# Seven-product MLPs: VectorE takes GpSimd's arithmetic, GpSimd issues the stores, four products share a pair of banks

## The chip, the cores and the metric

The kernel runs on one core of a Trainium2 chip. The core has a matrix engine (TensorE, PE in the rows; PEld is its weight load), three engines for elementwise work (VectorE, DVE; ScalarE, ACT; GpSimd, POOL) and SyncE (SP), which only issues transfers. TensorE writes its sums to banks of PSUM, from where VectorE and ScalarE take them to SBUF. Each engine works through its own list of instructions in order; an instruction that has to wait holds up all behind it on that engine, transfers it issues among them. The metric is the time of one execution in microseconds. Three executions before took 1092.06, 1092.88 and 1094.47 us.

## The reference

Causal attention (4 batches, 8 heads, 576 positions, 64 per head) gives x of 2304 tokens by 512. Two MLPs follow, the second on the output of the first:

```python
def _moe_ref(x, w_in, w_out):          # 512 -> 2048 -> 512
    h = x @ w_in
    r = np.maximum(h, 0.0)
    g = r * r
    return (g @ w_out).astype(np.float32)

def _moe2_ref(x, w_in, w_out):         # 512 -> 2048 -> 512
    h = x @ w_in
    g = np.maximum(0.01 * h, h)        # leaky, slope 0.01
    return (g @ w_out).astype(np.float32)
```

The weights are given as 64-bit floats, inputs and output otherwise as 32-bit ones.

## The kernel before

There are five stages: attention with the first product of the first MLP (`up1`, plain) running beside and behind it, then three stages by seven products: `down` (g by w_out of MLP 1), `up` (by w_in of MLP 2) and `out` (by w_out of MLP 2).

**Seven products.** A block of 512 by 512 weights and a block of 512 rows by 768 tokens are each seen as 2 by 2 sub-blocks, and seven products of sums and differences of sub-blocks take the place of eight. Tokens go in three super-blocks (sb) of 768; the 2048-wide dimension goes in four quarters q. In `down` and `out` the loop is sb, product, q: the four q add up in PSUM, so a product is closed after four steps. In `up` it is sb, q, product: each product is closed after one step. A step is one call of `multiply` (L800): 12 matmuls of 384 columns in `down` and `up`, 18 of 256 in `out` (L792 in the rows). Each operand and each weight is cut into a rounded part and a rest, hence three passes.

**Operands.** `Operands.make` (L884) makes the operand of a step: ScalarE rounds (L889), VectorE forms the rest (L890), 768 elements in each of 128 partitions. Behind some products the sub-blocks are combined for later ones: L892 and L895 on VectorE, L894 and L897 on GpSimd, so four subtractions for each (sb, q) beside the seven rests. `down` makes three steps ahead (LEAD), in a ring of four buffers.

**Weights.** A 64-bit weight becomes a 32-bit one in `convert`: load into `wst` (SP, L140 or L142), L111 and L113 on ScalarE, L112 on VectorE, an integer addition L115 on GpSimd, L116 on VectorE, store to `wscr` (SP, L170). `wst` has one buffer in each stage, so the next load waits for L116. `arrive` reads four sub-blocks back, forms sums on GpSimd (L203 to L212) and cuts them for the products (L182 ScalarE, L183 VectorE). These are jobs that are started at numbered ticks, one tick for each step: the 16 conversions for `up` every third tick of `down`, those for `out` every second tick of `up`.

**Outputs.** `Outputs.done` (L840) is called when a product is closed. A product adds into a pair of banks, CHAIN says which: products 1 and 2 share one pair, 5 and 3 one, 7 and 4 one, 6 has its own. For each group of seven, ScalarE copies twice from PSUM (L844, L856) and VectorE adds five times (L848 to L863), and in `up` VectorE applies the slope to each of four outputs (L868). The stores (L955, L961, L966) are issued by SP, as all loads are. There are four pairs of banks, handed out in turn.

**Order.** A scheduler lays each engine's instructions in the order of its own estimate of the times; matmuls keep the order of the program. The buffers of a stage lie on those of the stage before in the order in which `open_pools` names them, and a buffer waits for what lay there. In `out` the first operand takes `dop1`, which lies on `cpost`, the buffers from which the last outputs of `up` are stored.

## Time and profile before

| | us |
|---|---|
| median of three executions | 1092.88 |
| the profiled execution | 1096.18 |
| its span, first to last instruction | 1094.3 |
| PE busy | 980.6 (90%) |
| DVE busy | 805.9 (74%) |
| ACT busy | 586.7 (54%) |
| POOL busy | 417.6 (38%) |

The matmuls of `down` begin at 459.4 us, those of `up` at 683.4, those of `out` at 903.0, and the last ends at 1089.9. Attention and `up1` fill what lies before. A busy share says little here, since every engine is in a different place of the program in each stage: the stages are read one by one, and in each the question is what PE waited for. In rows of waits, `A <- B` means that engine A stood idle until B ended.

### The profile page before, as it was taken

The numbers are of one execution on the slowest core, as the hardware profiler recorded it, in microseconds if no ns is written. First come the engines' busy times: TensorE is split into PE (matmuls) and PEld (weight loads), VectorE is DVE, ScalarE is ACT, GpSimd is POOL, SyncE is SP. The second block draws the span as 40 slices with busy tenths as digits, with TensorE's granted clock in tenths as the row PEclk, the third lists the DMA queues.
The fourth block names the chain that finished last, engine by engine and source line by source line (L and its number), as shares of the span: only waits on it lengthen the run. The fifth ranks groups of instructions, "written<-read, shape, count | busy, mean of one in ns | idle before, by whom it ended". The sixth has DMA issues, their size and how long they took to land.

```text
span 1094.3 us, 17158 instructions
## 1 busy us (share of the span) xinstructions
PE 980.6 (90%) x6056; PEld 886.3 (81%) x6056; DVE 805.9 (74%) x1299; ACT 586.7 (54%) x1149; POOL 417.6 (38%) x393
## 2 busy tenths in 40 slices
PE   5988999999999998889798787988988949999998
PEld 4766777888788777879688687887988949999998
DVE  6688776855777343396976979899688986696874
ACT  5577787877888566554444435443233433434432
POOL 4466555322552043234523434453123531232320
PEclk9899999999999999999999999999998988999999
DMA  7554747352745567757448243666757662624401
GB/s 138 120 127 117 174 148 176 111 144 65 179 149 167 196 223 260 254 182 255 134 151 278 91 159 126 216 216 200 238 164 237 215 207 84 208 72 140 150 3 57
DMA packets 206413, 178.53 MB, mean 163 GB/s; under 512 B 101460, under 2 KB 182356, under 8 KB 206328
## 3 DMA queue, kind: packets, MB, share of 16 engines
q1 hardware_dynamic: 193072, 158.26, 49.0%
q10 hardware_dynamic: 13256, 19.18, 4.8%
q8 instruction: 48, 0.79, 0.3%
q14 instruction: 37, 0.30, 0.1%
HBM read 111.25 MB, written 66.13 MB: 162 GB/s over the span
## 4 chain that ended last, share of the span: by engine, by line
PE 35%; DVE 24%; DMA 18%; issue 10%; ACT 8%; POOL 2%; SPq 1%; ACTq 0%; DVEq 0%; POOLq 0%
PE q L792 20%; PE h L602 7%; DMA wst<-in_moe_w_in_dram 6%; DVE op L890 6%; DMA wst<-in_moe_w_out_dram 4%; PE tr L514 3%; DVE wt L116 3%; DMA wb<-wscr 3%; DVE post L868 2%; DVE w L183 2%; PE tr L474 2%; PE S L424 2%; DVE t L440 2%; ACT wst L113 1%; ACT t L464 1%
## 5 line engine op out<-in xcount | busy, mean ns | idle before, releaser
L792 PE MATMUL q<-op,w 128*128 128x384 f32 x2016 | 375.6, 345 | 57.3 <-DVE op L890 30.5
L792 PEld LDWEIGHTS q<-op,w 128*128 128x128 f32 x2016 | 359.5, 193 | 73.3 <-DVE op L890 39.5
L890 DVE TENSOR_TENSOR op<-gp,op 128x768 fp32r<-128x768 f32 x189 | 234.5, 1255 | 53.3 <-ACT op L889 53.2
L602 PE MATMUL h<-xs,w 128*128 128x512 f32 (+1 forms) x960 | 232.1, 386 | 15.5 <-ACT r L588 6.8
L889 ACT ACTIVATE op<-gp 128x768 fp32r<-128x768 f32 x189 | 154.3, 841 | 161.0 <-PE q L792 121.9
L602 PEld LDWEIGHTS h<-xs,w 128*128 128x128 f32 x960 | 164.0, 195 | 47.2 <-ACT r L588 9.6
L792 PE MATMUL q<-w,op 128*128 128x256 f32 x1512 | 185.1, 286 | 13.2 <-ACT op L889 11.4
L792 PEld LDWEIGHTS q<-w,op 128*128 128x128 f32 x1512 | 184.1, 194 | 14.3 <-ACT op L889 11.7
L115 POOL TENSOR_TENSOR wt<-wt,wst 128x512 uint32<-128x512 uint32 x64 | 90.3, 1412 | 204.6 <-ACT wst L113 143.2
L111 ACT ACTIVATE wt<-wst 128x512 f32<-128x512 f32 x64 | 42.7, 667 | 139.1 <-DMA wst<-in_moe_w_in_dram 82.8
L897 POOL TENSOR_TENSOR gp<-gp 128x768 f32<-128x768 f32 x27 | 59.7, 2223 | 108.8 <-DVE op L890 105.0
L464 ACT ACTIVATE t<-t,m 128x128 f32<-128x128 f32 (+2 forms) x144 | 83.4, 580 | 32.5 <-DVE m L440 30.3
L894 POOL TENSOR_TENSOR gp<-gp 128x768 f32<-128x768 f32 x27 | 61.9, 2299 | 79.7 <-DVE gp L892 40.1
L112 DVE TENSOR_SCALAR wt<-wt 128x512 uint32<-128x512 uint32 x64 | 34.6, 541 | 68.3 <-ACT wt L111 68.3
L440 DVE CUSTOM_DVE_ANT_0 t<-S,mask 128x128 f32<-128x128 f32 (+2 forms) x129 | 57.7, 476 | 22.1 <-PE S L424 12.5
L474 PE MATMUL tr<-ident,t 128*128 128x128 f32 x384 | 67.4, 286 | 5.2 <-ACT t L464 3.2
L739 DVE TENSOR_TENSOR pT<-tr,pT 128x384 fp32r<-128x384 f32 (+2 forms) x96 | 51.6, 550 | 22.7 <-ACT pT L732 22.2
L474 PEld LDWEIGHTS tr<-ident,t 128*128 128x128 f32 x384 | 46.4, 144 | 21.5 <-issue 5.2
L116 DVE SCALAR_TENSOR_TENSOR wt<-wst,wt 128x512 uint32<-128x512 uint32 x64 | 51.7, 808 | 14.0 <-POOL wt L115 14.0
L868 DVE SCALAR_TENSOR_TENSOR post<-post 128x768 f32<-128x768 f32 x48 | 59.2, 1242 | 0.3
L732 ACT ACTIVATE pT<-tr 128x384 fp32r<-128x384 f32 (+4 forms) x108 | 51.1, 485 | 13.9 <-PE tr L474 11.6
L387 POOL TENSOR_TENSOR Y<-yt,Y 128x576 fp32r<-128x576 f32 x30 | 43.0, 1441 | 26.2 <-ACT Y L386 26.0
(103 smaller groups left out, 1225.7 us busy)
## 6 DMA issues: line engine op xcount, KB each, us to landing
gp<-gscr SPq DMA_DIRECT2D x48, 384.0 KB
qscr<-post SPq DMA_DIRECT2D x48, 384.0 KB
gp<-qscr SPq DMA_DIRECT2D x48, 384.0 KB
wst<-in_moe_w_in_dram SPq DMA_DIRECT2D x32, 512.0 KB
gscr<-gs ACTq DMA_DIRECT2D x32, 512.0 KB
wst<-in_moe_w_out_dram SPq DMA_DIRECT2D x32, 512.0 KB
wscr<-wt SPq DMA_DIRECT2D x48, 256.0 KB
wb<-wscr SPq DMA_DIRECT2D x40, 256.0 KB
```

The costliest lines, as they stand in the source:

```text
L115: nc.gpsimd.tensor_tensor(t, t, lw, ALU.add)
L116: nc.vector.scalar_tensor_tensor(t, hw, 0xC0000000, t, ALU.bitwise_and, ALU.bitwise_or)
L440: return nc.vector.tensor_tensor_reduce(t[:, a:z], sc, msk, -QK_SCALE, first, ALU.add, ALU.min, m).ins
L464: done = nc.scalar.activation(t[:, a:z], t[:, a:z], AF.Exp, bias=m[:, c:c + 1], scale=-1.0, accum_out=sums[:, s0:s0 + 1])
L474: nc.tensor.transpose(tr[:, c * P:(c + 1) * P], t[:, c * P:(c + 1) * P], ident)
L602: nc.tensor.matmul(h[:, :w], win[fc][:, a, c * P:(c + 1) * P], xs[j, c][:, z, :w], start=(c == 0 and y == 0), stop=(c == KC - 1 and y == 2))
L792: i = nc.tensor.matmul(*args, skip_group_check=True, **kw).ins
L868: nc.vector.scalar_tensor_tensor(t[1], t[1], 0.01, t[1], ALU.mult, ALU.max)
L889: a = nc.scalar.activation(t[:, 0], src, AF.Copy)
L890: c = nc.vector.tensor_tensor(t[:, 1], src, f32(t[:, 0]), ALU.subtract)
L894: nc.gpsimd.tensor_tensor(b[0, 1], b[1, 1], b[0, 1], ALU.subtract)
L897: nc.gpsimd.tensor_tensor(b[1, 0], b[1, 0], b[0, 0], ALU.subtract)
```

## The change

In the three stages by seven products, GpSimd no longer computes: the subtractions for operands, those for weights and the integer addition of `convert` go to VectorE, the stores of outputs and converted weights and one weight load in each `arrive` go from SP to GpSimd. The products are taken in another order and with other intermediate sums: 1, 7, 6, 2, 5, 4, 3. Products 1, 6, 5 and 3 now add into one pair of banks one after another, 7 and 4 into a second, 2 into a third; after 1, 6 and 7 ScalarE copies the state so far, after 2, 5 and 4 VectorE adds the copy, after 3 ScalarE takes the result. The slope is an activation of ScalarE. Conversions start every fourth tick in `down` (14 of them) and every third in `up` (18), and the buffers of `up` and `out` are named in another order: the first operand of `out` now lies on `cwa`, where weights are staged in `up`. The functions `convert` and `arrive` also make the weights of `down` beside attention and `up1` (16 conversions, 4 arrivals), so their additions, sums and stores move there as well.

```diff
-    ORDER = (1, 5, 6, 7, 2, 3, 4)
-    CHAIN = {1: 0, 2: 0, 5: 1, 3: 1, 6: 2, 7: 3, 4: 3}
-    FIRST = (1, 5, 6, 7)
-    EARLY = (1, 5, 6, 7)
+    ORDER = (1, 7, 6, 2, 5, 4, 3)
+    CHAIN = {1: 0, 6: 0, 5: 0, 3: 0, 7: 1, 4: 1, 2: 2}
+    FIRST = (1, 7, 2)
+    EARLY = (1, 7, 6, 5)
...
-    def words(t, st):
+    def words(t, st, adder=nc.gpsimd):
...
-        nc.gpsimd.tensor_tensor(t, t, lw, ALU.add)
+        adder.tensor_tensor(t, t, lw, ALU.add)
...
-    def convert(mat, ch, stage):
+    def convert(mat, ch, stage, adder=nc.vector):
...
-        yield from words(t, st)
-        yield
-        nc.sync.dma_start(wscr[mat][ch], f32(t))
+        for _ in words(t, st, adder):
+            pass
+        yield
+        nc.gpsimd.dma_start(wscr[mat][ch], f32(t))
...
-        def fetch(t, m, k):
+        def fetch(t, m, k, queue=nc.sync):
...
-            nc.sync.dma_start(t, wscr[mat][4 * q + b:4 * q + 4:2, :, h * 2 * P:(h + 1) * 2 * P]
+            queue.dma_start(t, wscr[mat][4 * q + b:4 * q + 4:2, :, h * 2 * P:(h + 1) * 2 * P]
...
         yield
         yield
         for i in ORDER:
-            if i == 5:
-                nc.gpsimd.tensor_tensor(s, c, u, ALU.add)
-                nc.gpsimd.tensor_tensor(c, a, c, ALU.subtract)
+            if i == 7:
+                nc.vector.tensor_tensor(s, c, u, ALU.add)
+                nc.vector.tensor_tensor(c, a, c, ALU.subtract)
             if i == 6:
-                nc.gpsimd.tensor_tensor(s, s, a, ALU.subtract)
-            if i == 7 and (keep or 2 in products):
-                fetch(a, 0, 1)
-            if i == 2:
+                nc.vector.tensor_tensor(a, s, a, ALU.subtract)
+            if i == 2 and (keep or 2 in products):
+                fetch(c, 0, 1, nc.gpsimd)
                 yield
-                if keep or 3 in products:
-                    nc.gpsimd.tensor_tensor(s, a, s, ALU.subtract)
+            if i == 3 and (keep or 3 in products):
+                nc.vector.tensor_tensor(c, c, a, ALU.subtract)
             if i not in products:
                 continue
             w = weight_tile(mat, i, q)
-            cut([w[:, z] for z in range(2)], {1: a, 5: s, 6: s, 7: c, 2: a, 3: s, 4: u}[i])
+            cut([w[:, z] for z in range(2)], {1: a, 7: c, 6: a, 2: c, 5: s, 4: u, 3: c}[i])
             yield
         if keep:
             yield
-            nc.sync.dma_start(sscr[q], s.rearrange("p c e -> p (c e)"))
+            nc.gpsimd.dma_start(sscr[q], c.rearrange("p c e -> p (c e)"))
     def arrive_kept(i, stage):
...
-        opens, closes = i in FIRST, i not in (1, 5, 7)
+        opens = i in FIRST
...
-            self.acc, self.ended = {}, []
+            self.acc, self.kept, self.ended = {}, {}, []
...
+        def leak(self, out, src):
+            nc.scalar.activation(out, src, AF.Prelu, alpha=0.01)
...
-            if i == 1:
-                self.s1, s1 = self.temp()
-                nc.scalar.activation(s1, x, AF.Copy)
-                self.s1v = s1
-            elif i == 6:
-                self.u2 = self.temp()
-                nc.vector.tensor_tensor(self.u2[1], y, self.s1v, ALU.add)
-                self.s5 = self.temp()
-                nc.vector.tensor_tensor(self.s5[1], z, self.u2[1], ALU.add)
-            elif i == 7:
-                nc.vector.tensor_tensor(self.s5[1], w, self.s5[1], ALU.add)
-                self.end(where, 1, 1, self.s5)
-            elif i == 2:
+            acc = self.view(self.acc[CHAIN[i]])
+            if i in (1, 6, 7):
                 t = self.temp()
-                nc.scalar.activation(t[1], x, AF.Copy)
-                self.end(where, 0, 0, t)
+                nc.scalar.activation(t[1], acc, AF.Copy)
+                self.kept[i] = t
             elif i == 3:
                 t = self.temp()
-                nc.vector.tensor_tensor(t[1], z, self.u2[1], ALU.add)
-                self.end(where, 0, 1, t)
-            elif i == 4:
-                nc.vector.tensor_tensor(self.u2[1], w, self.u2[1], ALU.add)
-                self.end(where, 1, 0, self.u2)
-        def end(self, where, m, h, t):
-            if self.kind == "up":
-                nc.vector.scalar_tensor_tensor(t[1], t[1], 0.01, t[1], ALU.mult, ALU.max)
-            self.ended.append((self.finish, where, m, h, t[0], t[1]))
+                if self.kind == "up":
+                    self.leak(t[1], acc)
+                else:
+                    nc.scalar.activation(t[1], acc, AF.Copy)
+                self.ended.append((self.finish, where, 0, 1, *t))
+            else:
+                t = self.kept.pop({2: 1, 5: 7, 4: 6}[i])
+                nc.vector.tensor_tensor(t[1], acc, t[1], ALU.add)
+                if self.kind == "up":
+                    self.leak(t[1], t[1])
+                self.ended.append((self.finish, where, {2: 0, 5: 1, 4: 1}[i], {2: 0, 5: 1, 4: 0}[i], *t))
     class Operands:
...
         def make(self, sb, q, i):
             b = {(k, h): self.part[sb, q, k, h] for k in range(2) for h in range(2)}
-            src = {1: b[0, 0], 5: b[0, 0], 6: b[0, 0], 7: b[0, 1], 2: b[1, 0], 3: b[1, 1], 4: b[1, 0]}[i]
+            src = b[{1: (0, 0), 7: (0, 1), 6: (0, 1), 2: (1, 0), 5: (0, 0), 4: (1, 0), 3: (1, 1)}[i]]
+            if i == 7:
+                nc.vector.tensor_tensor(b[0, 1], b[1, 1], b[0, 1], ALU.subtract)
             t = self.new(i)
             with tc.high_priority():
                 a = nc.scalar.activation(t[:, 0], src, AF.Copy)
                 c = nc.vector.tensor_tensor(t[:, 1], src, f32(t[:, 0]), ALU.subtract)
             if i == 1:
                 nc.vector.tensor_tensor(b[0, 0], b[0, 1], b[0, 0], ALU.subtract)
-            if i == 5:
-                nc.gpsimd.tensor_tensor(b[0, 1], b[1, 1], b[0, 1], ALU.subtract)
-                nc.vector.tensor_tensor(b[0, 0], b[1, 1], b[0, 0], ALU.subtract)
+            if i == 7:
+                nc.vector.tensor_tensor(b[0, 1], b[1, 1], b[0, 0], ALU.subtract)
             if i == 2:
-                nc.gpsimd.tensor_tensor(b[1, 0], b[1, 0], b[0, 0], ALU.subtract)
+                nc.vector.tensor_tensor(b[1, 0], b[1, 0], b[0, 1], ALU.subtract)
             self.op[sb, q, i] = t
             return a.ins, c.ins
...
-                    nxt = {2: (0, 0), 7: (0, 1), 3: (1, 1), 4: (1, 0)}.get(mi)
+                    nxt = {5: (0, 0), 2: (0, 1), 3: (1, 1), 4: (1, 0)}.get(mi)
...
-        nc.sync.dma_start(zscr[2 * m:2 * m + 2, :, n:n + HN].rearrange("c p n -> p c n"), t)
+        nc.gpsimd.dma_start(zscr[2 * m:2 * m + 2, :, n:n + HN].rearrange("c p n -> p c n"), t)
...
-        nc.sync.dma_start(qscr[4 * q + m:4 * q + 4:2, :, n:n + HN].rearrange("f p n -> p f n"), t)
+        nc.gpsimd.dma_start(qscr[4 * q + m:4 * q + 4:2, :, n:n + HN].rearrange("f p n -> p f n"), t)
...
-        nc.sync.dma_start(out[n:n + HN, m * 2 * P:(m + 1) * 2 * P].rearrange("(t p) e -> p t e", p=P),
+        nc.gpsimd.dma_start(out[n:n + HN, m * 2 * P:(m + 1) * 2 * P].rearrange("(t p) e -> p t e", p=P),
...
-        for ch in range(FC):
-            jobs.add(16 + 3 * ch, convert, 1, ch, stage)
-        jobs.add(70, arrive, 1, 0, stage, ORDER)
+        for ch in range(FC - 2):
+            jobs.add(14 + 4 * ch, convert, 1, ch, stage)
+        jobs.add(71, arrive, 1, 0, stage, ORDER)
...
-        b = open_pools(stack, ("c23", "cwa", "cwst", "c15", "cy", "c4", "cpost", "c67", "cwt"))
+        b = open_pools(stack, ("c62", "c54", "cwst", "c17", "cy", "cpost", "c3", "cwa", "cwt"))
...
-        at_op = {2: "c23", 3: "c23", 6: "c67", 7: "c67", 1: "c15", 5: "c15", 4: "c4"}
+        at_op = {x: name for name in ("c62", "c54", "c17", "c3") for x in map(int, name[1:])}
...
+        for ch in range(FC - 2, FC):
+            jobs.add(4 * (ch + 2 - FC), convert, 1, ch, stage)
...
-            jobs.add(24 + 2 * ch, convert, 2, ch, stage)
+            jobs.add(10 + 3 * ch, convert, 2, ch, stage)
...
-        b = open_pools(stack, ("d11", "dpost", "dpad", "d01", "d00", "d10", "dop1", "dop0"))
+        b = open_pools(stack, ("d01", "d11", "dpad", "dop0", "d00", "d10", "dpost", "dop1"))
```

What this does to the order is shown in three places. First VectorE in the second super-block of `down`, where the operands of products 1 and 5 (before) and 1 and 7 (after) are made. Before:

```order
L892 TENSOR_TENSOR gp<-gp 128x768
L890 TENSOR_TENSOR op<-gp,op 128x768
L112 TENSOR_SCALAR wt<-wt 128x512
L892 TENSOR_TENSOR gp<-gp 128x768
L890 TENSOR_TENSOR op<-gp,op 128x768 x2
L895 TENSOR_TENSOR gp<-gp 128x768
L116 SCALAR_TENSOR_TENSOR wt<-wst,wt 128x512
L895 TENSOR_TENSOR gp<-gp 128x768
L890 TENSOR_TENSOR op<-gp,op 128x768 x2
L895 TENSOR_TENSOR gp<-gp 128x768 x2
```

After; L884 is the rest of an operand, L886, L880 and L888 are the combinations, L115 the integer addition:

```order
L886 TENSOR_TENSOR gp<-gp 128x768
L884 TENSOR_TENSOR op<-gp,op 128x768
L115 ISA wt<-wst,wt 128x1024
L884 TENSOR_TENSOR op<-gp,op 128x768
L880 TENSOR_TENSOR gp<-gp 128x768
L886 TENSOR_TENSOR gp<-gp 128x768
L116 SCALAR_TENSOR_TENSOR wt<-wst,wt 128x512
L884 TENSOR_TENSOR op<-gp,op 128x768
L888 TENSOR_TENSOR gp<-gp 128x768
L880 TENSOR_TENSOR gp<-gp 128x768
L884 TENSOR_TENSOR op<-gp,op 128x768
L888 TENSOR_TENSOR gp<-gp 128x768
```

The two combinations that GpSimd made (L894 and L897 are not in VectorE's rows before) now stand among the operands, and so does L115.

Second, ScalarE in the later part of `up`. `post` is an output buffer, `q` with a number a pair of banks. Before, one pair of copies from PSUM in each group of seven (L844, L856), with a conversion (L111, L113) behind each:

```order
L844 ACTIVATE post_8113<-q_8099 128x768
L111 ACTIVATE wt_8213<-wst_8176 128x512
L113 ACTIVATE wst_8176<-wst_8176 128x512
L856 ACTIVATE post_8191<-q_8099 128x768
L111 ACTIVATE wt_8253<-wst_8217 128x512
L113 ACTIVATE wst_8217<-wst_8217 128x512
L844 ACTIVATE post_8251<-q_8237 128x768
L111 ACTIVATE wt_8292<-wst_8257 128x512
L113 ACTIVATE wst_8257<-wst_8257 128x512
L856 ACTIVATE post_8329<-q_8237 128x768
```

After, the copies L847 of products 1, 7 and 6 of one group and the first slope (L829), with cuts of weights (L183) and a conversion between; 8642 is the shared pair:

```order
L847 ACTIVATE post_8656<-q_8642 128x768
L183 ACTIVATE w1_8737<-wb_8694 128x512
L183 ACTIVATE w3_8734<-wb_8564 128x512
L847 ACTIVATE post_8672<-q_8659 128x768
L183 ACTIVATE w7_8757<-wb_8694 128x512
L111 ACTIVATE wt_8482<-wst_8443 128x512
L113 ACTIVATE wst_8443<-wst_8443 128x512
L847 ACTIVATE post_8689<-q_8642 128x768
L183 ACTIVATE w6_8776<-wb_8694 128x512
L183 ACTIVATE w2_8811<-wb_8694 128x512
L829 ACTIVATE post_8656<-post_8656 128x768
L183 ACTIVATE w5_8828<-wa_8696 128x512
```

The copy of product 6 stands behind the conversion's L111, and the next product on that pair, 5, must wait for it.

Third, SP's transfers in `up`. Before, stores of outputs (L961) and of converted weights (L170) between the loads of weights (L140):

```order
L140 DMA wst<-in_moe_w_out_dram 128x1024
L170 DMA wscr_73<-wt 128x512
L961 DMA qscr<-post 128x2x384 x3
L140 DMA wst<-in_moe_w_out_dram 128x1024
L170 DMA wscr_73<-wt 128x512
L961 DMA qscr<-post 128x2x384
L140 DMA wst<-in_moe_w_out_dram 128x1024
L170 DMA wscr_73<-wt 128x512
L961 DMA qscr<-post 128x2x384 x3
L140 DMA wst<-in_moe_w_out_dram 128x1024
```

After, at the place where the loads of the last weights begin, loads alone:

```order
L142 DMA wst<-in_moe_w_in_dram 128x4x256 x2
L192 DMA wb<-wscr_72 128x2x256
L140 DMA wst<-in_moe_w_out_dram 128x1024
L192 DMA wb<-wscr_72 128x2x256
L192 DMA wa<-wscr_72 128x2x256
L140 DMA wst<-in_moe_w_out_dram 128x1024 x3
L192 DMA wb<-wscr_73 128x2x256 x2
L140 DMA wst<-in_moe_w_out_dram 128x1024
```

and the stores on GpSimd's list (L954 outputs, L171 converted weights, L192 the load that moved):

```order
L954 DMA qscr<-post 128x2x384
L192 DMA wb<-wscr_72 128x2x256
L171 DMA wscr_73<-wt 128x512
L954 DMA qscr<-post 128x2x384 x3
L171 DMA wscr_73<-wt 128x512
L954 DMA qscr<-post 128x2x384
```

## Rows read from the trace of the kernel before

**Rows 1.** Windows by stage: us, busy time (and count) of each engine, clock, DMA share, GB/s.

```profile
0.00:459.00 459.00, 419.89 (x2528) 342.66 (x2528) 286.31 (x786) 328.73 (x791) 196.08 (x274) 0.97 0.57 159
459.00:681.00 222.00, 189.28 (x1022) 179.26 (x1022) 188.23 (x177) 102.46 (x146) 90.65 (x45) 0.98 0.55 177
683.50:891.60 208.10, 186.18 (x994) 180.21 (x994) 182.57 (x209) 79.97 (x123) 76.64 (x49) 0.95 0.66 213
903.00:1090.00 187.00, 185.09 (x1512) 184.11 (x1512) 134.96 (x119) 72.75 (x87) 46.36 (x22) 0.98 0.33 102
```

**Rows 2.** Waits in `down`: total us, times, longest.

```profile
PE q L792 <- DVE op L890: 29.3, 22, 3.3
...
DVE wt L112 <- ACT wt L111: 23.2, 9, 4.8
```

**Rows 3.** Lines of VectorE: ns min/median/max; L890 in `down` alone.

```profile
L890 DVE TENSOR_TENSOR op<-gp,op x90: 941/949/2603, 459.4 to 679.1; 128x768 fp32r<-128x768 f32 x90
...
L848 DVE TENSOR_TENSOR post<-q,post x18: 943/948/958, 494.3 to 1055.4; 128x768 f32<-128x768 f32 x18
...
L116 DVE SCALAR_TENSOR_TENSOR wt<-wst,wt x64: 649/680/2329, 48.5 to 863.5; 128x512 uint32<-128x512 uint32 x64
```

**Rows 4.** Groups of VectorE in `down`: count, busy us, mean ns, idle before.

```profile
L890 DVE TENSOR_TENSOR op<-gp,op 128x768 fp32r<-128x768 f32 x84 | 112.1, 1357 | 9.0 <-ACT op L889 8.9
```

**Rows 5.** Timeline in `out`: start, us, engine, line; [idle before].

```profile
906.49 1.82 DVE L892 TENSOR_TENSOR gp<-gp 128x768 f32<-128x768 f32 x2
...
939.18 1.85 POOL L897 TENSOR_TENSOR gp<-gp 128x768 f32<-128x768 f32 x1 [0.90 <-DVE op L890]
...
939.72 2.12 DVE L890 TENSOR_TENSOR op<-gp,op 128x768 fp32r<-128x768 f32 x1 [0.62 <-ACT op L889]
```

**Rows 6.** Waits in `up`, SP's own transfers last.

```profile
PE q L792 <- DVE post L850: 16.5, 9, 3.1
...
ACT wt L111 <- DMA wst<-in_moe_w_out_dram: 49.7, 15, 5.5
...
SPq L961 <- DVE post L868: 71.2, 35, 5.1
```

**Rows 7.** Timeline of one conversion in `up`.

```profile
794.38 0.67 ACT L111 ACTIVATE wt<-wst 128x512 f32<-128x512 f32 x1 [5.51 <-DMA wst<-in_moe_w_out_dram]
...
795.08 0.43 DVE L112 TENSOR_SCALAR wt<-wt 128x512 uint32<-128x512 uint32 x1 [4.02 <-ACT wt L111]
...
795.42 0.95 DVE L848 TENSOR_TENSOR post<-q,post 128x768 f32<-128x768 f32 x1
...
795.70 1.30 POOL L115 TENSOR_TENSOR wt<-wt,wst 128x512 uint32<-128x512 uint32 x1 [6.23 <-ACT wst L113]
...
798.64 16.41 PE L792 MATMUL q<-op,w 128*128 128x384 f32 x84 [2.31 <-DVE post L850]
...
801.86 0.67 ACT L111 ACTIVATE wt<-wst 128x512 f32<-128x512 f32 x1 [4.68 <-DMA wst<-in_moe_w_out_dram]
```

**Rows 8.** Timeline of PE in `up`: an undisturbed run of seven steps.

```profile
730.12 14.80 PE L792 MATMUL q<-op,w 128*128 128x384 f32 x84 [1.28 <-DVE post L850]
```

**Rows 9.** Window in `up` behind a pause of 3.1 us.

```profile
835.00:840.00 5.00, 5.00 (x16) 5.00 (x17) 3.73 (x5) 1.91 (x3) 1.86 (x2) 0.50 1.01 382
```

**Rows 10.** Timeline between `up` and `out`.

```profile
892.45 9.92 SPq L961 DMA_DIRECT2D qscr<-post  x3
...
902.14 0.84 ACT L889 ACTIVATE op<-gp 128x768 fp32r<-128x768 f32 x1 [7.93 <-DMA qscr<-post]
...
903.03 0.58 PE L792 MATMUL q<-w,op 128*128 128x256 f32 x1 [11.42 <-ACT op L889]
```

**Rows 11.** Groups of ScalarE, whole program.

```profile
L844 ACT ACTIVATE post<-q 128x768 f32<-128x768 f32 x18 | 14.3, 797 | 4.2 <-PE q L792 3.2 <-ACT w L182 1.0
```

**Rows 12.** Timeline of the last steps.

```profile
1081.31 0.96 DVE L860 TENSOR_TENSOR post<-q,post 128x768 f32<-128x768 f32 x1 [0.28 <-PE q L792]
...
1089.95 0.96 DVE L863 TENSOR_TENSOR post<-q,post 128x768 f32<-128x768 f32 x1 [6.75 <-PE q L792]
```

1 line of the change is left out of this document (removed).

## The prediction

> **What bounds the kernel now.** I read the windows by stage first, for where PE falls short, then the waits of the stages, then a timeline of one such wait, then durations with and without GpSimd beside them.
>
> [rows 8] show a run that nothing stopped: 84 matmuls in 14.80 us, 0.176 us each, so a step of `down` or `up` is 12 x 0.176 = 2.11 us, and the 1008 matmuls of either stage (3 sb x 4 q x 7 x 12) are 177.6 us. `down` took 222.0 and `up` 208.1 [rows 1]: 44.4 and 30.5 us too much. `out` had PE busy in 185.1 of 187.0 us [rows 1] and has little to give, but before it PE stood still for 11.4 us [rows 10]. In `down` the pauses of PE belong to VectorE's operands, 29.3 us in 22 waits [rows 2]; in `up` to VectorE's additions from PSUM, 16.5 us in 9 [rows 6]. The rest of the excess is slow matmuls behind pauses: in the 5 us behind one of 3.1 us the granted clock was 0.50, the lower of the two levels (1.2 GHz), and 16 matmuls ran where 0.176 would give 28 [rows 9].
>
> Two causes stand behind VectorE's lateness. The first is GpSimd. The rest of an operand took 941 ns at least, 949 in the median and up to 2603 [rows 3], mean 1357 [rows 4]; the timeline shows a long one, 2.12 us, that runs into an operation of GpSimd [rows 5]. Additions with one input in PSUM and one in SBUF keep to 943 to 958 ns in all 18 cases [rows 3]. So over 84 operands of `down` GpSimd cost 112.1 - 84 x 0.949 = 32 us of VectorE. This is what the Trainium skill says (page "SBUF — State Buffer", section "Who interferes with whom"): a VectorE instruction with two SBUF inputs contends with a GpSimd one that reads SBUF, one with at most one SBUF input does not; these rows agree. The second cause is a conversion that stands in the way. ScalarE stood 5.51 us before L111 until the load had landed, VectorE 4.02 before L112, and only behind it came L848 and L850, for which PE waited 2.31 us [rows 7]. L111 waited 49.7 us so in `up` [rows 6], and in `down` VectorE stood 23.2 us before L112 [rows 2]. A conversion came every 7.5 us (794.38 to 801.86 in [rows 7]), but was asked for every 4.2 us in `up` (two ticks) and every 6.3 in `down` (three). SP, which issues the next load, stood 71.2 us of `up` before stores of outputs [rows 6].
>
> **The change part by part.**
>
> *`down`, VectorE's work.* Two subtractions back to back took 1.82 us, the second starting 0.87 behind the first [rows 5]; that is the price of one of 768 elements when its input is there. Seven rests and four combinations, where two of the latter come from GpSimd: 12 x 11 x 0.87 = 115 us. Three additions from PSUM in each sb in place of five: 9 x 0.87 = 8. Of the 512-wide work, 12 cuts of kept weights and 11 cuts and sums of the first `arrive` at 0.68 [rows 3] (L116, the nearest row with two inputs): 16. A conversion: 0.43 for L112 [rows 7], 0.68 for L116 [rows 3], and the integer addition, which VectorE does not show before. Its bounds are 0.68 (the same 512 words with two inputs in L116) and, since the order prints 1024 elements for it, twice that, 1.36. I take 0.8, nearer the first, since the words are the same; 14 x 1.9 = 27. The sum is 166 us against 177.6 of PE. Before, VectorE was busy for 188 of 222 [rows 1]. It no longer sets the pace in the mean, but it does in bursts: products 1 and 7 want 4 x 2 x 0.87 + 4 x 3 x 0.87 = 17.4 us, with two conversions 21.2, in the 16.9 us of their eight steps. With three steps made ahead, less the 1.8 us that an operand itself takes, that costs 0 to 2 us in the second and third sb. At the start nothing is made ahead and the 12 cuts come on top: 17.4 + 8.2 = 25.6 against 16.9, 8 us.
>
> *`down`, conversions.* Asked for every 8.4 us (four ticks), and shorter than the 7.5 of now by GpSimd's 1.30 [rows 7] less 0.8: 7.0. They no longer fall behind, so the 23 us before L112 should go. Together I leave `down` 12 us of waits and 6 of lower clock, 18 of 44.4: **26 us gained**. Bounds: 0 if VectorE stays as slow as now, 38 if only 6 remain.
>
> *`up`.* VectorE loses 48 slopes and 24 additions and gets 28 sums for weights, 18 integer additions and 6 subtractions; by the same prices 36 additions and 33 operand operations are 60, 18 conversions 34 and 77 operations on weights 52 us: 146 of 177.6. ScalarE rises from 80 [rows 1] by 12 more copies and 48 slopes at about 0.80 [rows 11] to some 128. Neither is the bound; the order is. A copy starts 0.28 us behind its product [rows 12] and takes 0.80 [rows 11], and the next product on the same pair waits for it: 6 for 1, 5 for 6, 3 for 5, and in the next group 7 for 3, each with one product, 2.11 us, between. So 1.0 us may be lost in ScalarE's list before PE stops, at 48 places. Before, two products or more lay between. What can be lost there is the wait for a weight load: a conversion of 7.0 us is now asked for every 6.3, so it falls behind by about 0.7 each, 13 us over 18. I leave `up` 13 us of waits and 5 of clock, 18 of 30.5: **12 us gained**. Bounds: 46 us lost (below) and 24 gained.
>
> The Trainium skill (page "Perfetto Trace Analysis", section "Optimizing Tensor Performance") wants independent groups of matmuls to rotate through different banks, so that one is emptied while the next is computed; that rule speaks against one pair for four products. Here another pair's product lies between in each case, which the row of 0.80 us covers; by the rule alone `up` would lose, and that is the second rival.
>
> *`up` to `out`.* ScalarE's first operand of `out` waited 7.93 us for a store of an output, and PE 11.42 [rows 10]. Its buffer now lies on staged weights. The last of these is cut behind the slope of product 3: 0.28 + 0.80, then 0.53 for the cut (512 elements in place of 768 of a copy of 0.80), then the operand's two parts, 0.84 [rows 10] and 0.95 [rows 3]: 3.4 us in all, and 0.6 for hand-overs: 4. **7 us gained**; bounds 0 and 11.
>
> *The rest.* `out` gets 24 subtractions of VectorE, 21 us, on 135 of 187 busy [rows 1], beside matmuls: nothing, bounds 3 us either way. Before `down`, 16 integer additions and 16 sums, 22 to 33 us, go to VectorE, which is busy for 286 of 459 us [rows 1] where PE is busy for 420: nothing, bounds 8 us either way. The end: 0.95 us for the last addition [rows 12] against 0.80 for a copy, but a store that GpSimd issues, which no row shows; 0 to 3 us, I take **1 us lost**. The moved stores themselves I cost at nothing: six output buffers in `up` are used again seven products, 15 us, after their store is issued. If GpSimd fell behind by more than that, PE would wait for buffers.
>
> Sum: 26 + 12 + 7 - 1 = 44. The profiled execution took 1096.18 us for a span of 1094.3, 3.3 above the median of 1092.88 but made the same way; I take the 44 us off the median: **1049 us**.
>
> **The rivals.**
>
> *GpSimd's transfers slow VectorE as its arithmetic did* (A). For it: GpSimd still works beside every operand, and no row shows a transfer issued there. Against it: the slow cases have two readers of SBUF, and a store reads through the transfer engines. Price: 32 us over the 38 GpSimd operations of `down` (22 subtractions in its window, 16 additions) is 0.85, with the slower others some 1.1 us each. 27 transfers in `down` put 30 us on 166: 196, and with the bursts it gains 17; 73 in `up` put 80 on 146: 226, and it loses 18 or so. Sum 17 - 18 + 7 - 1 = 5 gained: 1088.
>
> *The shared pair waits for ScalarE* (B), the slower side. The conversion still stands in ScalarE's list between copies, as the order of `up` shows. If L111 goes on waiting as now (49.7 / 15 = 3.3 us each [rows 6]) and stands before a copy with 1.0 us to spare, PE stops for 2.3 us at each of 18 conversions, 41 us, and each such pause is followed by slow matmuls: 12 lost at half the rate in 5 us [rows 9], about 2 us, 36 in all. `up` then has 77 us in place of 30.5: 26 - 46 + 7 - 1 = 14 lost, 1107. It decides from 3.5 us a conversion upwards, where 18 of them eat the 30.5 and the 32 gained elsewhere. Against it: loads no longer stand behind stores on SP, and the spacing asked for is wider.
>
> *Nearly all waits go* (C). With VectorE at 0.87 and loads on time, 8 us remain in `down` and 8 in `up`: 36 + 22 + 9 = 67 gained, 1026. Against it: the first eight steps of `down` alone cost about 8.
>
> That the slopes and subtractions do not leave GpSimd is ruled out by the order. That the integer addition takes 1.36 costs up to 8 us in `down` and 6 in `up`, which lies in the forecast's own range.
>
> **How the numbers follow.** The forecast, 1035 to 1066 in its own range, has 0.54; A 0.14, B 0.16, C 0.16. A range of 1024 to 1092 leaves out B and a little of A and of C. No change means within 0.2%, 2 us, about what repeated runs of this kernel can tell. Faster: forecast, C and most of A, 0.80; same: a part of A, 0.05; slower: B, less its mild end, with a little of A, 0.15.
>
> **What would show it.** Right: rests of operands near 0.95 us throughout with GpSimd issuing only transfers; no pause of over 2 us in `down` beyond its first eight steps; L111's waits in `up` under 2 us in the mean; PE's pause before `out` of about 4 us, ended by an operand and not by a store. Wrong: PE waiting for L847 or L829 over 20 us in `up` (B); operands of 1.5 us and more beside transfers of GpSimd (A); VectorE busy over 95% of `down`; or a longer stretch before `down`.

## The result and the profile after

| | before | changed |
|---|---|---|
| median (of 4 executions each), us | 1092.47 | 1050.19 |
| lowest to highest, us | 1089.87 to 1094.47 | 1046.97 to 1053.28 |
| changed over before | | 0.9614, 95% interval 0.9576 to 0.9653 |
| the profiled execution, and its span, us | 1096.18, 1094.3 | 1051.8, 1050.0 |

The forecast was 1049. Windows by stage of the changed kernel (us, busy time and count of PE, PEld, VectorE, ScalarE and GpSimd, clock, DMA share, GB/s), which answer to [rows 1]:

```profile
0.00:459.40 459.40, 420.67 (x2528) 344.48 (x2528) 300.10 (x817) 328.61 (x792) 169.05 (x266) 0.97 0.57 159
459.50:653.46 193.96, 181.42 (x1009) 175.88 (x1010) 167.05 (x213) 104.30 (x146) 16.91 (x27) 0.99 0.60 195
653.48:854.20 200.72, 182.75 (x1009) 175.40 (x1007) 135.97 (x195) 126.38 (x188) 48.97 (x73) 0.99 0.69 227
858.90:1044.60 185.70, 184.35 (x1512) 183.99 (x1512) 126.78 (x137) 76.11 (x93) 8.29 (x11) 0.98 0.35 107
```

For the stages I count matmuls: `up` begins with the 1009th of 2016. [rows 1] let 14 matmuls of `up` stand in `down` (1022), so by this count `down` took 219.1 us before and `up` 213.1. The profiled executions, in us:

| | before | changed | gained | forecast |
|---|---|---|---|---|
| up to `down` | 459.4 | 459.5 | 0 | 0 |
| `down` | 219.1 | 193.9 | 25.2 | 26 |
| `up` | 213.1 | 200.7 | 12.4 | 12 |
| pause before `out` | 11.4 | 4.8 | 6.6 | 7 |
| `out` | 186.9 | 185.7 | 1.2 | 0 |
| behind the last matmul | 4.4 | 5.4 | -1.0 | -1 |

GpSimd computes nothing in these stages now; what its column counts are the issues of transfers. In the rows of the changed kernel L883 and L884 make an operand (rounded part on ScalarE, rest on VectorE), L847 is a copy from PSUM, L858 VectorE's addition from PSUM, L829 the slope, and L183 and L184 cut weights. The lines of VectorE in the whole program (ns, least, median and most) and the group of rests in `down`, as in [rows 3, 4]:

```profile
L884 DVE TENSOR_TENSOR op<-gp,op x189: 946/955/960, 459.5 to 1036.9; 128x768 fp32r<-128x768 f32 x189
...
L115 DVE CUSTOM_DVE_ANT_0 wt<-wst,wt x48: 679/692/1917, 273.0 to 825.6; 128x1024 uint16<-128x1024 uint16 x48
```
```profile
L884 DVE TENSOR_TENSOR op<-gp,op 128x768 fp32r<-128x768 f32 x89 | 83.2, 953 | 3.2 <-ACT op L883 2.8
```

The mean rest fell from 1357 to 953 ns, and the longest of all 189 is 960, beside a GpSimd that issues transfers: 53 of the 189 overlap such an issue in the trace, and none of these is longer. The integer addition takes as long as a two-input operation of 512 words, the lower of its two bounds. What is waited for in `down` and then in `up` (total, times, longest), which answers to [rows 2, 6]:

```profile
ACT wt L111 <- DMA wst<-in_moe_w_in_dram: 38.9, 13, 5.5
DVE wt L112 <- ACT wt L111: 19.1, 11, 4.1
...
PE q L792 <- DVE op L884: 10.8, 13, 2.8
```
```profile
DVE wt L112 <- ACT wt L111: 37.6, 17, 5.1
ACT wt L111 <- DMA wst<-in_moe_w_out_dram: 32.9, 16, 4.5
...
PE q L792 <- ACT post L847: 8.2, 11, 1.6
PE q L792 <- DVE post L858: 7.2, 6, 2.9
...
ACT wt L111 <- DMA wst<-in_moe_w_in_dram: 4.3, 2, 2.4
```

PE's waits for operands in `down` fell from 29.3 to 10.8 us. The waits for weights have hardly gone: 19.1 us of VectorE in `down` (23.2 before), and 37.2 of ScalarE in `up` (49.7). One such place in `up`, in order of time:

```profile
775.72 0.66 ACT L111 ACTIVATE wt<-wst 128x512 f32<-128x512 f32 x1 [3.15 <-DMA wst<-in_moe_w_out_dram]
...
776.85 0.84 ACT L829 ACTIVATE post<-post 128x768 f32<-128x768 f32 x1
...
779.01 1.50 ACT L847 ACTIVATE post<-q 128x768 f32<-128x768 f32 x2
...
779.86 1.33 PE L792 MATMUL q<-op,w 128*128 128x384 f32 x6 [1.56 <-ACT post L847]
```

ScalarE stood 3.15 us before the conversion, the copies came behind it, and PE stood 1.56 us for a shared bank. Last, the step from `up` to `out`, as in [rows 10]:

```profile
856.69 0.63 ACT L183 ACTIVATE w<-wb 128x512 fp32r<-128x512 f32 x1 [1.59 <-DVE wb L212]
...
858.08 1.58 ACT L883 ACTIVATE op<-gp 128x768 fp32r<-128x768 f32 x2 [0.76 <-DVE w L184]
...
858.97 0.38 PE L792 MATMUL q<-w,op 128*128 128x256 f32 x1 [4.77 <-ACT op L883]
```

The first operand waits for the last cut of staged weights, no longer for a store.

### The profile page after: what moved, and what is told of

The parts are those of the page before. It is cut to its first block, busy times and chain, and to the rows that moved or that the text cites. A ratio compares the mean times of both kernels' runs of the same rounds, so it can differ in the third digit from the quotient of the medians.

```text
span 1050.0 us, 17100 instructions
## 1 busy us (share of the span) xinstructions
PE 969.3 (92%) x6056; PEld 879.8 (84%) x6056; DVE 733.2 (70%) x1365; ACT 638.6 (61%) x1221; POOL 245.4 (23%) x379
## 3 DMA queue, kind: packets, MB, share of 16 engines
q1 hardware_dynamic: 161200, 113.16, 39.5%
q0 software_dynamic: 13184, 45.10, 11.1%
## 5 line engine op out<-in xcount | busy, mean ns | idle before, releaser
L792 PE MATMUL q<-op,w 128*128 128x384 f32 x2016 | 364.2, 339 | 30.9 <-DVE op L884 12.5
L792 PEld LDWEIGHTS q<-op,w 128*128 128x128 f32 x2016 | 351.3, 189 | 43.7 <-DVE op L884 17.3
L883 ACT ACTIVATE op<-gp 128x768 fp32r<-128x768 f32 x189 | 155.7, 842 | 134.7 <-PE q L792 108.8
L884 DVE TENSOR_TENSOR op<-gp,op 128x768 fp32r<-128x768 f32 x189 | 178.5, 955 | 53.8 <-ACT op L883 53.0
L111 ACT ACTIVATE wt<-wst 128x512 f32<-128x512 f32 x64 | 42.5, 665 | 94.3 <-DMA wst<-in_moe_w_in_dram 59.9
L112 DVE TENSOR_SCALAR wt<-wt 128x512 uint32<-128x512 uint32 x64 | 28.0, 438 | 88.4 <-ACT wt L111 88.3
L171 POOL DMA_DIRECT2D wscr<-wt x48 | 27.1, 564 | 215.3 <-DVE wt L116 210.0
L440 DVE CUSTOM_DVE_ANT_0 t<-S,mask 128x128 f32<-128x128 f32 (+2 forms) x129 | 57.6, 476 | 23.1 <-PE S L424 12.7
L739 DVE TENSOR_TENSOR pT<-tr,pT 128x384 fp32r<-128x384 f32 (+2 forms) x96 | 51.4, 550 | 16.3 <-ACT pT L732 15.8
L732 ACT ACTIVATE pT<-tr 128x384 fp32r<-128x384 f32 (+4 forms) x108 | 51.3, 487 | 16.3 <-PE tr L474 13.4
L184 DVE TENSOR_TENSOR w<-wb,w 128x512 fp32r<-128x512 f32 x58 | 39.2, 688 | 29.9 <-ACT w L183 29.6
L858 DVE TENSOR_TENSOR post<-q,post 128x768 f32<-128x768 f32 x54 | 51.5, 954 | 9.8 <-PE q L792 8.3
L116 DVE SCALAR_TENSOR_TENSOR wt<-wst,wt 128x512 uint32<-128x512 uint32 x64 | 49.3, 770 | 7.4 <-POOL wt L115 6.8
L588 ACT ACTIVATE r<-h 128x512 f32<-128x512 f32 (+1 forms) x80 | 43.7, 548 | 17.4 <-PE h L602 15.4
L954 POOL DMA_DIRECT2D qscr<-post x48 | 34.3, 716 | 83.8 <-ACT post L829 83.4
```

The lines of the kernel that those rows point to most:

```text
L116: nc.vector.scalar_tensor_tensor(t, hw, 0xC0000000, t, ALU.bitwise_and, ALU.bitwise_or)
L440: return nc.vector.tensor_tensor_reduce(t[:, a:z], sc, msk, -QK_SCALE, first, ALU.add, ALU.min, m).ins
L588: nc.scalar.activation(r[:, :w], h[:, :w], AF.Relu)
L732: nc.scalar.activation(out[0], src, AF.Copy)
L739: nc.vector.tensor_tensor(out[1], src, f32(out[0]), ALU.subtract)
L792: i = nc.tensor.matmul(*args, skip_group_check=True, **kw).ins
```

## The experiments

Ratios are to the kernel before, timed on the same chip, with 95% intervals. The changed kernel's is 0.9614.

### Which engines compute

**Two subtractions back on GpSimd.**

```diff
-                nc.vector.tensor_tensor(b[0, 1], b[1, 1], b[0, 1], ALU.subtract)
+                nc.gpsimd.tensor_tensor(b[0, 1], b[1, 1], b[0, 1], ALU.subtract)
...
-                nc.vector.tensor_tensor(b[1, 0], b[1, 0], b[0, 1], ALU.subtract)
+                nc.gpsimd.tensor_tensor(b[1, 0], b[1, 0], b[0, 1], ALU.subtract)
```

> The changed kernel, with two of the four subtractions that combine operand blocks (first of product 7, and the one behind product 2) computed by GpSimd again, as before the change; all else as changed. Theory (GpSimd's arithmetic slows VectorE's two-input work): the rests of operands (L884), 0.95 us each in all 189 cases of the changed kernel, go back to 1.2 to 1.4 us in the mean in `down`, with single ones over 2 us; `down` takes 207 to 222 us in place of 201, the whole 1056 to 1075. Rival (the gain came from the new chain and the fewer waits for weights, and VectorE is now relieved of 26 subtractions): rests stay at 0.95 us, `down` 196 to 203, the whole 1044 to 1053.

Measured: 1069.74 us, 0.978 (0.974 to 0.982). Groups of VectorE from 455 to 675 us, then two neighbours in time:

```profile
L884 DVE TENSOR_TENSOR op<-gp,op 128x768 fp32r<-128x768 f32 x89 | 99.6, 1135 | 10.3 <-ACT op L883 9.9
```
```profile
533.55 2.44 POOL L880 TENSOR_TENSOR gp<-gp 128x768 f32<-128x768 f32 x1 [0.95 <-DVE gp L886]
534.21 2.06 DVE L112 TENSOR_SCALAR wt<-wt 128x512 uint32<-128x512 uint32 x1
```

The theory holds: two subtractions of the eleven operations for each (sb, q) cost 19 us, though VectorE has less to do; `down` took 215.7 us. The rests' mean, 1.14, lies a little under the 1.2 expected. L112, which has one input and takes 0.43 us alone, took 2.06 beside GpSimd.

**Only the engines of the arithmetic, on the kernel before.** Every `nc.gpsimd.tensor_tensor` of the stages by seven products and of `convert` becomes `nc.vector.tensor_tensor`.

> The kernel before, with only the arithmetic of GpSimd in the stages by seven products (subtractions of operands, sums of weights, 48 integer additions) moved to VectorE; order of products, banks, slope, stores and spacing as before. Theory (the largest part of the gain is VectorE no longer being slowed): L890 falls from a mean of 1.36 to 0.95 us in `down`, `down` falls from 222 to between 203 and 214 and the whole to 1066 to 1082. Rival (the chain and the wider spacing made the gain; VectorE only gets more to do): `down` 218 to 228, the whole 1085 to 1100.

Measured: 1066.27 us, 0.9742 (0.9703 to 0.978). Windows of `down`, of PE's pause behind it and of `up`, then PE's row there and the group of rests from 455 to 640 us:

```profile
454.00:636.00 182.00, 176.82 (x1006) 174.19 (x1007) 163.14 (x205) 97.14 (x134) 0.00 (x0) 1.00 0.61 198
636.00:662.50 26.50, 0.53 (x4) 0.21 (x2) 12.36 (x18) 7.74 (x13) 0.00 (x0) 0.55 0.69 230
662.50:863.90 201.40, 183.49 (x1008) 175.42 (x1008) 185.50 (x254) 78.34 (x122) 0.00 (x0) 0.99 0.65 207
```
```profile
662.56 6.35 PE L792 MATMUL q<-op,w 128*128 128x384 f32 x24 [26.03 <-ACT w L182]
```
```profile
L890 DVE TENSOR_TENSOR op<-gp,op 128x768 fp32r<-128x768 f32 x90 | 84.2, 952 | 8.8 <-ACT op L889 8.7
```

This edit alone gives 28 us, and the rests are back at 0.95. From its first matmul to its last `down` fell to 182 us, 4 above its matmuls, further than the theory had it; but the 16 conversions don't end in so short a stage (the last began at 656.0 us, the matmuls of `down` end at 636.5), and PE stood 26 us for the first weights of `up`.

**Everything but the engines.** The changed kernel with arithmetic, slope and stores on the engines of before.

> The changed kernel with every engine as before: two subtractions of operands, the sums of weights and the integer additions on GpSimd, the slope on VectorE, all stores on SP. What is left of the change is the order of products, the shared banks, the spacing of conversions and the layout of buffers. Theory (VectorE's speed makes most of the gain): rests of operands 1.2 to 1.4 us in `down`, `down` 212 to 222, PE's pause before `out` 4 to 6 us by the layout alone, the whole 1070 to 1088. Rival (order, banks and spacing make most of it): `down` 200 to 208, the whole 1050 to 1065.

Measured: 1103.44 us, 1.008 (1.0049 to 1.011): slower than either expectation, and than before. Rests took 1.25 us in the mean. Without the moves between engines the new order, banks, spacing and layout together are worth nothing; the run doesn't tell them apart.

**The slope on VectorE.**

```diff
-            nc.scalar.activation(out, src, AF.Prelu, alpha=0.01)
+            nc.vector.scalar_tensor_tensor(out, src, 0.01, src, ALU.mult, ALU.max)
...
-                    self.leak(t[1], acc)
+                    nc.scalar.activation(t[1], acc, AF.Copy)
+                    self.leak(t[1], t[1])
```

> The changed kernel with the leaky slope on VectorE as before the change (48 operations L830 of one SBUF operand read twice; after product 3 ScalarE copies first). Theory of the forecast (VectorE has room in `up`, 131 of 194 us busy, and the slope is not what the gain rests on): VectorE gets 48 x 0.87 = 42 us more, stays under 175 us in `up`, and the whole is 1050 to 1060, as VectorE's additions from PSUM, for which PE waited 7 us, come later by 0.9 now and then. Rival (the slope off VectorE is a main part of the gain in `up`): `up` 200 to 210, the whole 1058 to 1068.

Measured: 1067.57 us, 0.974 (0.9698 to 0.9783). The rival holds: 17 us. `up` took 205.4 us, 4.7 more; the larger part lies behind it, where PE's pause before `out` grew from 4.8 to 21.0 us. The last converted weights were stored only at 854.7 us (827.9 in the changed kernel), so they were read back and cut behind the end of `up`. PE where `out` begins (line numbers are one higher in this run):

```profile
877.23 0.58 PE L792 MATMUL q<-w,op 128*128 128x256 f32 x1 [20.97 <-ACT op L884]
```

### Which queue stores stand on

**All stores on SP.** `nc.gpsimd.dma_start` becomes `nc.sync.dma_start` in five places, and `fetch(c, 0, 1, nc.gpsimd)` loses its queue.

> The changed kernel with all stores, and the one load of each arrival, issued by SP again instead of GpSimd; arithmetic as changed. Theory (stores on SP hold up the loads of weights behind them, so that conversions start late): ScalarE's wait before L111 in `up` rises from 37 us to 45 to 60, `up` takes 197 to 206 us in place of 193.7, the whole 1053 to 1064, of which the tail gives 1 us back. Rival (which queue stores stand on costs nothing): within 2 us of 1050, or 1 us faster by the tail.

Measured: 1038.32 us, 0.9491 (0.9461 to 0.9522). Both expectations fell: it is 12 us faster than the changed kernel. In its profile `down` took 193.6 us (193.9 in the changed kernel), `up` 188.0 (200.7), the pause before `out` 12.0 (4.8). That execution took 1044.11 us, the longest of four, so its stages account for 8 of the 12 us. Waits in `up`:

```profile
ACT wt L111 <- DMA wst<-in_moe_w_out_dram: 12.7, 13, 1.9
...
ACT wt L111 <- DMA wst<-in_moe_w_in_dram: 3.7, 2, 1.9
...
PE q L792 <- ACT post L847: 1.8, 4, 0.6
...
PE q L792 <- DVE post L858: 0.2, 1, 0.2
```

With the same arithmetic, ScalarE waits 16.4 us for loads in place of 37.2, and PE 2.0 for the banks in place of 15.4: the 12.7 us of `up`.

**Outputs' stores on SP, weights' on GpSimd.** `to_z`, `to_q` and `to_out` use `nc.sync`.

> The changed kernel with the stores of outputs (72 in the stages by seven products) issued by SP again; stores of converted weights, kept weights and the one load of each arrival stay on GpSimd. If the outputs' stores made the loss that all stores on SP took back: 1036 to 1043. If the weights' stores and loads made it: 1047 to 1053. If both share it: between.

Measured: 1047.09 us, 0.956 (0.952 to 0.9599); `up` 197.0 us, the pause before `out` 4.8. By the expectation's ranges the weights' transfers made most of the loss.

**All stores on SP, the one load of each arrival on GpSimd.**

> The changed kernel with all stores issued by SP, and only the one load of each arrival (third sub-block pair of weights) on GpSimd, as in the change. With all on SP the whole was 1038 us, but PE's pause before `out` 12.0 us in place of 4.8, since this load stood behind stores of outputs on SP. Theory: the pause falls back to 4 to 6 us, the rest stays as with all on SP, the whole 1029 to 1034. Rival (the last loads of operands, not this one, set the pause): still 10 to 12 us, the whole 1036 to 1041.

Measured: 1036.8 us, 0.947 (0.9436 to 0.9505); `up` 191.3 us, the pause before `out` 10.3, so the rival holds for it. With the run before: the outputs' stores on GpSimd cost some 3 us (with intervals that overlap), the 52 stores of weights some 10.

**The work of a conversion a tick later.** One more `yield` in `convert` ahead of `words`; stores on GpSimd.

> The changed kernel, stores on GpSimd as changed, but in each conversion ScalarE's and VectorE's work (L111 to L116) starts one tick later behind the load. With the stores on SP the whole was 12 us faster than the changed kernel (1038 to 1050), and ScalarE's waits before L111 in `up` were 16 us against 37. Theory P (the scheduler, with other queues for the stores, places L111 too early in ScalarE's list, and copies stand behind it): with L111 a tick later its waits in `up` fall under 20 us, `up` from 193.7 to 187 to 191, the whole to 1038 to 1047. Rival Q (GpSimd's queue itself delays stores and loads): L111 waits less, but conversions then end later, `up` 192 to 198, the whole 1048 to 1056.

Measured: 1053.5 us, 0.9621 (0.9584 to 0.9657). Theory P fell: L111's waits in `up` were 30.5 us (37.2 in the changed kernel), PE's for the banks 15.7 (15.4). Rival Q's total fits, but its `up` does not (199.8 us), and `down` began 9 us sooner and took 9 longer, so the run settles no more than that.

### Where weights are loaded and where operands lie

**Two load buffers in `up`.**

```diff
-        stage, other = Stage(b["cwst"], b["cwt"], 1), Stage(b["cwa"], b["cwa"], 2)
+        stage, other = Stage(b["cwst"], b["cwt"], 2), Stage(b["cwa"], b["cwa"], 2)
...
-           Outputs("up", psum, b["cpost"], 6, to_q), jobs)
+           Outputs("up", psum, b["cpost"], 5, to_q), jobs)
```

> The changed kernel, stores on GpSimd as changed, but in `up` the weights of a conversion are loaded into two buffers in turn instead of one (an output buffer less makes room: 5 for 6), so a load no longer waits for the conversion before it. Over the kernels run so far, PE's waits for L847 and L858 in `up` rose with ScalarE's waits before L111: 2.0 us with 16.4, 5.5 with 20.7, 14 to 16 with 31 to 37. Theory (a conversion waiting for its load holds copies up, and the shared banks have 1 us to spare): L111's waits in `up` fall from 37 us to under 12, PE's waits for L847 and L858 from 15.4 us to under 5, `up` from 193.7 to 182 to 188, the whole to 1036 to 1045. Rival (the number of conversions, not their waits, or the missing output buffer): `up` 191 to 200, the whole 1047 to 1058.

Measured: 1063.12 us, 0.9723 (0.9684 to 0.9763). `up` 205.4 us. Neither as expected in the total, and the run does not decide cleanly: the larger buffer shifted the others, and PE stood where `up` begins. Waits from 690 us on, then that place:

```profile
ACT wst L113 <- DMA wst<-in_moe_w_out_dram: 19.2, 10, 3.2
...
PE q L792 <- ACT post L847: 6.0, 5, 2.5
...
PE q L792 <- DVE post L858: 3.4, 3, 1.2
```
```profile
659.46 0.69 PE L792 MATMUL q<-op,w 128*128 128x384 f32 x1 [9.10 <-ACT op L883]
...
667.84 0.57 PE L792 MATMUL q<-op,w 128*128 128x384 f32 x1 [2.84 <-ACT op L883]
```

The loads of the first operands of `up` were issued at 652 us there, at 621 in the changed kernel. Behind that place ScalarE's list has L113 ahead of L111, so a wait for a load stands at L113 there: 19.2 us, where L111 waited 37.2 in the changed kernel behind the same matmul. PE's waits for the banks are 9.4 in place of 15.4. Both fell, but the waits for loads were halved and not removed, so the run does not show how much of the 15 is theirs.

**Two load buffers in both stages, stores on SP.**

> The changed kernel with all stores on SP and two buffers in turn for the loads of conversions in `down` and in `up` (output buffers 3 for 4 and 5 for 6). With the stores on SP alone it was 1038 us, with PE waiting 5.3 us for weights where `up` begins and 12.0 before `out`, since conversions came every 9.8 and 8.5 us in place of the 8.4 and 6.3 asked for. Theory: conversions come as asked for, both pauses shrink to 1 and 5 us, `up` stays under 188: the whole 1022 to 1033. Rival (fewer output buffers make copies wait for stores on SP): 1036 to 1045.

Measured: 1042.74 us, 0.9538 (0.9497 to 0.9579). The time lies in the rival's range, but `up` begins as badly as in the run before, so it does not speak for the rival; and PE's longest row in `down` is

```profile
475.56 160.27 PE L792 MATMUL q<-op,w 128*128 128x384 f32 x923 [2.31 <-DVE op L884]
```

with no pause that the row shows, and there L111 no longer waits for a load, nor L112 for L111 (26.4 and 13.3 us in `down` with the stores on SP alone): what was left of `down` behind its start was conversions that wait for loads.

**The first operand of `out` on the outputs of `up`.** `dop1` and `d10` change places in the list of buffers.

> The changed kernel with two buffer regions of `out` exchanged: its first operand lies on the outputs of `up` again, as before the change, and the operands' sub-block b10 where weights were staged. Theory of the forecast (the layout takes the wait for an output's store away): PE's pause before `out` goes from 4.8 us to 8 to 12, the whole 1053 to 1058. Rival (the last arrival of weights, which stands ahead of the operand in ScalarE's list, sets the pause): still 4.8 us, the whole within 2 of 1050.

Measured: 1054.19 us, 0.9631 (0.9579 to 0.9682). ScalarE and PE where `out` begins:

```profile
859.18 0.84 ACT L883 ACTIVATE op<-gp 128x768 fp32r<-128x768 f32 x1 [3.41 <-DMA qscr<-post]
...
860.08 0.58 PE L792 MATMUL q<-w,op 128*128 128x256 f32 x1 [7.42 <-ACT op L883]
```

A store is waited for again, and the pause is 7.4 us, short of the 8 expected: the layout is worth 2.6 of the 6.6 us.

**A version from these.** Stores on SP, two load buffers in `down`, buffers renamed so that the first operands of `up` lie on blocks that are free early, and conversions at a pace they can keep. The edit of the pace (the others are left out):

```diff
-        for ch in range(FC - 2):
-            jobs.add(14 + 4 * ch, convert, 1, ch, stage)
+        for ch in range(FC):
+            jobs.add(12 + 18 * ch // 5, convert, 1, ch, stage)
...
-            jobs.add(10 + 3 * ch, convert, 2, ch, stage)
+            jobs.add(2 + 15 * ch // 4, convert, 2, ch, stage)
```

> The changed kernel with all stores on SP; two buffers in turn for the loads of conversions in `down` (3 output buffers there in place of 4), with the buffer regions of `down`, `up` and `out` named so that the first operands of `up` lie on the operand blocks of `down` that are free early, as in the changed kernel; and conversions spread over each stage at the pace they can keep: all 16 for `up` in `down`, every 3.6 ticks from tick 12, all 16 for `out` in `up`, every 3.75 ticks from tick 2. Two buffers gave `down` 923 matmuls in a row without a pause (160.3 us), but lost 20 to 25 us where `up` begins, by where its buffers lay. Theory (what is left of `down` and of the pauses at its end and before `out` is conversions that come late): `down` with the wait at its end 183 to 190 us in place of 194 with the stores on SP alone, `up` 185 to 191, the pause before `out` 4 to 8 us in place of 12, the whole 1020 to 1033. Rival (more conversions in the first part of `up` stand before the copies, or the new layout blocks `up` again): `up` over 195, the whole 1036 to 1050.

Measured: 1031.63 us, 0.9395 (0.9367 to 0.9423), the fastest of all. PE's rows:

```profile
468.70 0.69 PE L792 MATMUL q<-op,w 128*128 128x384 f32 x1 [12.06 <-ACT op L883]
469.69 16.80 PE L792 MATMUL q<-op,w 128*128 128x384 f32 x84 [0.31 <-DVE op L884]
487.00 168.75 PE L792 MATMUL q<-op,w 128*128 128x384 f32 x971 [0.51 <-DVE op L884]
```

`down` took 178.4 us, 1 us above its matmuls, and the first steps of `up` run through; `up` took 191.4 us, and the pause before `out` is 3.9. 12 us are lost ahead of `down`, where its first operands now load late. The theory holds for the whole time; of its parts `down` came out under its range, and `up` just over.

## Why the prediction was right, and where it was not

**GpSimd slows VectorE: right.** [rows 3 to 5] carried it. Rests went to 0.95 us, went back up to 1.14 with two subtractions on GpSimd, and were at 0.95 with the arithmetic alone moved, which gave 28 us. Rival A, that transfers slow VectorE as arithmetic does, is out: 946 to 960 ns in all 189 cases, 53 of them beside an issue. One sentence was too wide: I gave the rule of the Trainium skill (page "SBUF — State Buffer", section "Who interferes with whom") without its exception, an instruction with one input in a mode that uses both ports, for which it names `tensor_scalar`. L112 is one, and its 2.06 us in place of 0.43 beside GpSimd agree with the page.

**The start of `down`: right.** Its first 85 matmuls (15.0 us at 0.176) took 22.3, 7 lost where 8 was forecast.

**"They no longer fall behind, so the 23 us before L112 should go": wrong.** 19.1 us stayed. The pace was the error: the 7.5 us, and with them the 7.0, were read from one pair of conversions in `up`. From the first L111 of a stage to its last, a conversion came every 10.6 us before, in `down` as in `up`; in the changed kernel every 10.0 us in `down` (14 from 502.0 to 632.1) and every 8.7 in `up` (18 from 675.3 to 823.7), for the 8.4 and 6.3 asked for. The gain of `down` came out at 25.2 for 26 all the same; PE's waits for operands fell to 10.8 us, which fits a VectorE that catches up with rests of 0.95. What took these waits away was a second load buffer, with the stores on SP.

**`up`: right in size, in part by luck.** 12.4 us gained for 12. PE's waits for the banks were 15.4 us where I left 13, but the 13 came from a lateness of 0.7 us for each conversion, and the lateness was 2.4 (8.7 for 6.3). That is rival B's mechanism at a third of its price (41 us of pauses, without the slow matmuls behind): L111 waited 2.07 us in the mean (37.2 in 18) in place of 3.3, and 1.0 of that is slack. My sign of "under 2 us" for it was missed by a hair. The bounds of the stages helped, too: [rows 1] put `down` and `up` 44.4 and 30.5 us above their matmuls, where the count of matmuls gives 41.5 and 35.5. I left 18 in each; 16.3 and 23.1 are left. So `up` kept 5 us more than the sum had, and had begun 5 us higher.

**`up` to `out`: right in size, half right in cause.** The layout gave 2.6 of 6.6 us. For the rest, on the old layout a store was still waited for, but with GpSimd issuing it the pause was 7.4 us, and with SP (the kernel with only the arithmetic moved) 10.8; those two differ in more than the queue, and in the second the last weights came late and ScalarE waited only 0.93 us for the store, so this part is argued only. On the new layout the pause stayed at 4.8 with the outputs' stores on SP.

**"The moved stores themselves I cost at nothing": the step that failed.** Back on SP they make the kernel 12 us faster, so the rest of the change is worth about 55 us and the stores take 12 of it. In the sum this stood hidden: the 13 us of waits that I left in `up` as the price of the shared banks go to 2.0 with the stores on SP, where `up` gains 25 in place of 12; against it, the pause before `out` then gains nothing in place of 7. I had looked at whether buffers come free, not at what stands behind the stores' landing. The Trainium skill (page "SBUF — State Buffer", section "Summary: rules for kernel authors") advises to issue from ScalarE or SP transfers that run under VectorE's work, because GpSimd's own writing of descriptors is starved while VectorE is in one of its 2x or 4x modes; the advice agrees with these runs. The reason it gives is not seen: GpSimd's issues of the outputs of `up` stayed at one length.

```profile
L954 POOL DMA_DIRECT2D qscr<-post x48: 710/710/729, 668.0 to 855.4; - x48
```

What is seen is on SP, whose loads of arrivals wait for the stores of converted weights to land, 25.6 us in `up` with them on GpSimd and 12.4 with them on SP (changed kernel first):

```profile
SPq L192 <- DMA wscr<-wt: 25.6, 6, 5.7
```
```profile
SPq L192 <- DMA wscr<-wt: 12.4, 6, 3.9
```

Behind these loads stand those of the next conversion. This is a part of the 12 us at most: between the two runs that differ in the weights' stores alone lie 10 us, and SP waited so 17.7 us with them on GpSimd and 15.2 with them on SP. What makes the rest stays open, because each choice of queue also makes the scheduler lay ScalarE's and VectorE's instructions in another order, and no run held that fixed.

**What was not sized.** I put no price on the slope's move by itself; it is worth 17 us, since with the slope on VectorE the last weights came later. What is left of the change when every engine keeps its work (order, banks, spacing and layout) costs 8, and no run takes it apart. Rival C, nearly all waits gone at 1026, was not the changed kernel's case; the last version came within 6 us of it, with 12 lost ahead of `down`.

## What to carry to other kernels

Before an engine is relieved of work, look at what its work does to its neighbours: two subtractions for each operand group on an engine that had little else to do cost 19 us. Where converted data goes out and comes back, the store's queue is to be tried both ways: here it made 12 us, though the path is not shown. A pace read from one pair of places can mislead: 7.5 us there, 10.6 in the mean. When a stage gets shorter, jobs spread over it by a fixed count become the next bound, as the 26 us before `up` show where only the arithmetic was moved, and a buffer made larger shifts all that are laid out behind it.

## What the runs showed of the hardware

The integer addition on 1024 elements of 16 bits took 0.69 us, as long as an operation on 512 words of 32. What GpSimd issued (the stores, and one load of each arrival) went in larger packets than the same transfers by SP: 13184 packets for 45.1 MB in the changed kernel, where SP's queue had 31872 more for the same bytes with all of them on SP (193072 against 161200, 158.26 against 113.16 MB). Rows of the queues, changed kernel and then all stores on SP:

```profile
q1 hardware_dynamic: 161200, 113.16, 39.5%
q0 software_dynamic: 13184, 45.10, 11.1%
```
```profile
q1 hardware_dynamic: 193072, 158.26, 50.5%
```
